# Transnormer attention and a two-layer feed-forward: loads of batch 1, the place of GpSimd's first sums, and the queue of the tile loads

## The chip, the cores and the metric

The kernel runs on one core of a Trainium2 chip. TensorE (PE in the profile) multiplies, with its weight loads shown apart as PEld; VectorE is DVE, ScalarE is ACT, GpSimd is POOL, and SyncE (SP) computes nothing and issues DMAs. ScalarE and GpSimd can issue DMAs too. The metric is the device time of one execution in microseconds, the median over several runs.

## The reference

```python
def _attn_ref(q, k, v, g_norm):                 # (8, 8, 576, 64)
    kv = np.einsum('bhsd,bhse->bhde', k, v)
    out = np.einsum('bhsd,bhde->bhse', q, kv)
    rms = np.sqrt(np.mean(out * out, axis=-1, keepdims=True) + 1e-06)
    return (out / rms * g_norm).astype(np.float32)

def _moe_ref(x, w_in, w_out):                   # x (4608, 512), w_in (512, 2048)
    h = x @ w_in
    g = np.maximum(0.01 * h, h)
    return (g @ w_out).astype(np.float32)
```

The output of the attention, with heads and batch rearranged to 4608 rows of 512, is x. All arrays but the weights are float32. w_in and w_out are float64, so each of their tiles is loaded with twice the bytes and rounded to float32 on the chip.

## The kernel before

**Blocks.** The 4608 rows are taken as nine blocks of 512. The first block is computed plainly while the weights are still arriving; blocks 1 and 0 follow with one level of Strassen's scheme (block 0 for the half of the hidden columns that the first pass left out), and blocks 2 to 8 with two levels in the first product.

**Weight tiles.** There are 32 tiles of 512 KB (w_jobs), numbered in the order in which they are loaded and rounded. Tiles 0 to 15 belong to the first half of the hidden columns, 16 to 31 to the second half (16 to 19 and 24 to 27 are w_in, 20 to 23 and 28 to 31 are w_out, a chunk each). A tile of w_in takes four DMAs, one of w_out a single one. load_w issues them (L235), round_w and finish_w turn a tile into float32: two readings on ScalarE (L260, L262), a cut on VectorE (L264), one more on ScalarE (L269), and two operations on VectorE (L279, L282). The raw tiles lie in a few buffers (stage, pairs, early) that are used in turn.

**The first block** (L1112) has eight steps n. H n is the product with one w_in tile, O n the product with one w_out tile; H n needs tiles 0, 1, 3, 5, 7, 9, 11, 13 in this order, and O n needs tiles 2, 4, 6, 8, 10, 12, 14, 15. TensorE runs H 0, H 1, O 0, H 2, O 1 and so on. Between them `plan` (L1151) places, by hand, the rounding of tiles (numbers), the finishing of a tile (f), the steps of the attention of batch 1 (a: transposes of q, the product kv, its copy, the outputs o_ps, the norm) and the tail of batch 0 (t). Batch 1 is loaded as four pairs of heads; load_pair issues six DMAs for a pair (k, v and four pieces of q, 1,144 KB).

**Blocks 1 and 0** go by chunks c of 512 hidden columns, and a chunk has seven products in the order 1, 2, 6, 5, 7, 3, 4 (ORDER, L760). Products 1, 6, 7, 4 of the first layer accumulate in one PSUM bank (h_a or h_b), 2, and 5 with 3, in another (h_c or h_d): before a bank is accumulated on, its value must have been copied or added to g (done, L922: L925, L927, L932 and the adds of L697). The second layer's products o 1 to o 7 of a chunk run between the first layer's of the next chunk. A position in this run is a slot, seven to a chunk. GpSimd computes the sums that the scheme needs: of w_in (sides_w1, in `pairs`), of w_out (sides_w2), of g (sums_of, in gs), and a second level of w_in sums (combine, parts 0 and 1; part 2 is VectorE's). VectorE computes the sums of x (sides_x), all through add (L696). The sums of the weights are also written to DRAM (L750, L791 to L795), for the later blocks to read; a buffer in `pairs` is used again for the next chunk, so its sums wait until its write has landed.

**Order.** Most instructions are pinned, that is, they keep the order in which the program has them on their engine; the others the scheduler places when the kernel is built. GpSimd's first sum of a group is not pinned in blocks 1 and 0. Two small copies on GpSimd (L1178) that read x come ahead of its sums. In blocks 1 and 0 one tile is rounded at each of the slots of W_SLOTS, and the load of a later tile is issued there by ScalarE (L1284). Each DMA issued by SyncE or ScalarE carries one of eight semaphores in turn and waits for the DMA that carried it before.

Of the kernel before, what the change touches and what calls it, by code (L numbers as in the profile page):

```python
# [24 lines left out]
def kernel(  # L25
# [64 lines left out]
    ps_m = ctx.enter_context(tc.tile_pool(name="ps_m", bufs=1, space=bass.MemoryType.PSUM))  # L90

    pin = tc.keep_in_program_order
    steady = first_done = in_line = in_first = False

    def in_turn(ins):

# [56 lines left out]
    def load_pair(b, p, what="kvq", homes=None):  # L153


        if "k" in what:
            for i, (to, src) in enumerate(((k_ins, k), (v_ins, v))):
                to[b, p] = load_two(nc.sync, src[b, 2 * p:2 * p + 2],
                                    homes[i] if homes else in_tile("kv"[i]))
        if "q" not in what:  # L160
            return
        t = homes[2] if homes else ins.tile([P, T * D], F32, tag="q_in", name="q_in")
        for l in range(2):
            for c in range(2):
                r0, n = 64 * l + 32 * c, T * D - 32 * c
                src = q[b, 2 * p + half_of(p, l)].rearrange("(t s) d -> t (s d)", s=T)
                pin(nc.sync.dma_start(t[r0:r0 + 32, :n], src[:, 32 * c:]))
        q_ins[b, p] = t
# [131 lines left out]
    def load_w(j, *eng):  # L300
        eng = eng or (nc.sync,)
        dst, src = w_jobs[j]
        if w_in.dtype == I64:
            w_raws[j] = load_f64(src.bitcast(U32), eng)
        else:
            load(dst, src, eng)
# [7 lines left out]
    def round_w(j):  # L314

        steps = rounding(j)
        for _ in range(3):
            next(steps, None)
        finish_w()
        halfway.append(steps)  # L320
# [7 lines left out]
    def finish_w():  # L328
        while halfway:
            for _ in halfway.popleft():  # L330
                pass
# [214 lines left out]
    def first_attention():  # L546
# [43 lines left out]
        keep_warm(384)  # L590
        for j in range(3, 7):
            load_w(j)
        load_pair(1, 0)
        copy_kv(0, kv_ps)


# [74 lines left out]
        for _ in w0:  # L671
            pass
        load_w(7)
        load_pair(1, 1)
        invert(1)
        spread(1)
        w1 = rounding(1)
# [6 lines left out]
        halfway.append(w1)  # L684
        finish_w()
        load_w(8)
        load_pair(1, 2, homes=homes_1[2])
        for j in range(2, 5):
            round_w(j)
            load_w(j + 7)  # L690
            if j == 3:
                load_pair(1, 3, homes=homes_1[3])
        finish_w()


    def add(eng, out_, a, b_, minus=False, pinned=False):  # L696
        ins = eng.tensor_tensor(out_, a, b_, op=ALU.subtract if minus else ALU.add)  # L697
        if pinned or steady:
            pin(ins)

    def sides_w1(c):
# [22 lines left out]
    t12, t34 = pair(2, 2, U, N2), pair(3, 2, U, N2)  # L724
    writes = []

    def sides_w2(n):

        c = units[n][1]
        b11, b12 = w2_sb[0][c][:, :, :N2], w2_sb[0][c][:, :, N2:]
        b21, b22 = w2_sb[1][c][:, :, :N2], w2_sb[1][c][:, :, N2:]

        def sums(i):
            t = (t12, t34)[i]
            if n >= NC:
                pin(nc.sync.dma_start(t, w2_dram[c][i]))
                return
            if i == 0:  # L740
                add(nc.gpsimd, t[:, 0], b12, b11, True)
                add(nc.gpsimd, t[:, 1], b22, t[:, 0], True)
            else:
                add(nc.gpsimd, t[:, 0], b22, b12, True)
                add(nc.gpsimd, t[:, 1], b21, t12[:, 1], True)
            if (n, i) == (NC - 1, 1):

                writes.append((w2_dram[c][i], t))
            else:
                pin(nc.sync.dma_start(w2_dram[c][i], t))  # L750
        return {1: b11, 2: b21, 3: b22, 5: t12[:, 0], 6: t12[:, 1], 7: t34[:, 0],
                4: t34[:, 1]}, sums

# [16 lines left out]
    def combine(c, part):  # L770


        direct = w1_sb[0][c].rearrange("p u (t r) m -> p u r t m", t=2)
        last = w1_sb[1][c][:, :, 2:, :].unsqueeze(3)
        parts = [((5, 6), pair(0, U, 2, 2, P))], [((7, 3), pair(1, U, 2, 2, P))], \
            [((1, 2), direct), ((4,), last)]

        eng = nc.vector if part == 2 else nc.gpsimd
        for js, y in parts[part]:
            t = view(next(stage_homes), 0, 4, len(js), P)  # L780
            s1, s2, s3, s4 = (t[:, i, :, :] for i in range(4))
            y11, y12, y21, y22 = (y[:, u, r, :, :] for u in range(2) for r in range(2))

            add(eng, s1, y21, y22, pinned=part == 2)
            add(eng, s2, s1, y11, True, pinned=part == 2)
            add(eng, s3, y11, y21, True, pinned=part == 2)
            add(eng, s4, y12, s2, True, pinned=part == 2)
            to = w1_dram[c][:, :, AT[js[0]]:AT[js[0]] + len(js), :]
            if js[0] == 1:
                for r in range(2):  # L790
                    pin(nc.sync.dma_start(to[:, r, :, :], y[:, 0, r, :, :]))  # L791
            else:
                pin(nc.sync.dma_start(to[:, :2, :, :], y[:, 0, :, :, :]))
            pin(nc.sync.dma_start(to[:, 2, :, :], y22))
            pin(nc.sync.dma_start(to[:, 3:, :, :], t))  # L795


    reads = [(c, k) for _ in range(2, NB) for c in range(NC) for k in ORDER]
# [313 lines left out]
    def first_block(between):  # L1112
# [27 lines left out]
        for t in range(4):  # L1140
# [6 lines left out]

    first_attention()
    tail, a_steps = tail_of(0, NT, S, True), attention(1, False)
    t, a, f = "taf"  # L1150
    plan = {(1, 0): (t, 5), (1, 1): (t, t, 6, t), (2, 0): (t, 7, t), (2, 1): (t, f, a),  # L1151
            (3, 0): (a, 8), (3, 1): (f, a, 9), (4, 0): (10, f), (4, 1): (11,),
            (5, 0): (f, a, a, 12, a), (5, 1): (a, 13), (6, 0): (f, a, 14),
            (6, 1): (a, a, 15, a, f), (7, 0): (a, a), (7, 1): (16,), (8, 0): (f,)}
    loaded = 12

    def between(n, half):
        nonlocal loaded
        for what in plan.get((n, half), ()):
            if what == f:  # L1160
                finish_w()
            elif what in (t, a):
                go(tail if what == t else a_steps, 1)
            else:
                round_w(what)
                for j in range(loaded, {12: 17, 13: 18, 14: 19, 15: 20, 16: 21}.get(what, min(what + 7, 16)) + 1):
                    load_w(j)
                    loaded += 1
# [3 lines left out]
    in_first = False  # L1172
    first_done = True
    rounded = 17
    x_sides, _, sums, _ = sides_x(1)
    for _ in sums:
        pass
    for i, r in ((1, 0), (0, 1)):  # L1178
        nc.gpsimd.tensor_copy(pair(i, U, 2, 2, P)[:1, 0, 0, r, :1], x_sides[1][:1, 0, :1])
    h_sides, more = sides_w1(0)  # L1180
    more()
    for part in range(2):
# [33 lines left out]
    for i, chunks in rounds:  # L1216
# [7 lines left out]
        for c in chunks:  # L1224
# [5 lines left out]
            for t in range(7):  # L1230
# [30 lines left out]
                if slot in HELD and i == NB - 1:  # L1261
                    pass
                elif waited == LAG:
                    go_o()
                elif o_queue:
                    waited += 1
                if one:
                    at = 7 * now + t

                    if t == 1 and (i == 0 or c < K):  # L1270
                        combine(c, 2)
                    if t == 3 and nxt[0] < 2:
                        h_sides, more_h = sides_w1(nxt[1])
                        if nxt in ((1, 1), (0, K), (0, K + 1)):
                            combine(nxt[1], 0)
                    if t == 5 and nxt[0] < 2:
                        more_h()
                        if nxt in ((1, 1), (0, K), (0, K + 1)):
                            combine(nxt[1], 1)
                    if at in W_SLOTS:  # L1280
                        round_w(rounded)
                        rounded += 1
                        if loaded < len(w_jobs):
                            load_w(loaded, nc.scalar)  # L1284
                            loaded += 1
                    else:
                        finish_w()
                    if at in (19, 20):
                        load_pair(2, at - 19)
                    go(late, LATE_ONE.get(at, 0))  # L1290
                    go(a_steps, A_SLOTS.get(at, 0))
                    load_some()
                    if at in (33, 36):
                        for key in (("11", "12"), ("22", "21"))[at == 36]:
                            load_part(os, key)
                    if at == 7 * NC - 4:
                        x_sides, _, sums, _ = sides_x(0)
                        go(sums)
                    elif at == 7 * N1 - 4:
                        x_sides, new_quarters, sums, inner = sides_x(2)  # L1300
                        go(sums)
                    elif at == 7 * N1 - 3:
                        inner(0)
                    elif at == 7 * N1 - 2:
                        inner(1)
# [46 lines left out]
```

## Time and profile before

| | us |
|---|---|
| median of four runs | 946.19 (946.01 to 947.04) |
| the profiled execution, time | 946.01 |
| the profiled execution, span | 944.3 |

| Engine | busy us | share of the span |
|---|---|---|
| TensorE | 910.2 | 96% |
| its weight loads | 796.3 | 84% |
| VectorE | 638.2 | 68% |
| GpSimd | 391.8 | 41% |
| ScalarE | 346.9 | 37% |

The times in the text are microseconds from the span's start. In a timeline line the first number is the start and the second the duration; then come the engine (a q behind its name marks its DMA queue), the line of the code, the operation, what it writes and reads, and how many instructions are merged; in brackets stands how long the engine had stood still and what it waited for. In a line of waits stand who waited for whom, then the sum, how often, and the longest. TensorE's busy share by stretches shows where it stands still: from 0 to 100 us it is busy 90.3 us, from 100 to 200 us 80.4, and from 200 us on nearly throughout. The DMA engines are busy all the time from 15 to 45 and from 50 to 70 us (share 0.95 or more), and again from 96 to 124 us.

### The profile page before, as it was taken

What the parts mean: (1) busy time and instruction counts of PE and PEld (TensorE: products, weight loads), DVE (VectorE), ACT (ScalarE), POOL (GpSimd) and SP (SyncE); (2) the same over time, 40 slices, a digit from 0 to 9 for tenths busy, and PEclk for the clock granted to TensorE, in tenths of its full rate; (3) what the DMA queues carried; (4) which work ended last, traced back from release to release, by engine and by line L of the source; (5) the groups of instructions that cost most, each with busy time, mean ns of one, the idle gap of its engine ahead of it and who ended that gap; (6) DMA issues with size and microseconds to landing.
All of it is one profiled execution on the core that took longest, in us unless ns stands there. A gap on an engine that the chain in (4) does not pass through costs nothing.

```text
span 944.3 us, 18288 instructions
## 1 busy us (share of the span) xinstructions
PE 910.2 (96%) x7072; PEld 796.3 (84%) x7072; DVE 638.2 (68%) x1161; ACT 346.9 (37%) x682; POOL 391.8 (41%) x456
## 2 busy tenths in 40 slices
PE   9988598899999999999999999999999999999998
PEld 5533476788899899999999999999989999999997
DVE  5758577864665777578856876587758765755565
ACT  5645354412324432443234333433343333223231
POOL 2061555596423365225422452246224623452222
PEclk9999889999999999999999999999999999999999
DMA  8993973459788878877787779766865666667632
GB/s 266 249 239 103 350 221 123 144 165 296 251 248 300 251 223 216 263 242 220 222 261 226 242 210 269 232 202 195 256 193 174 189 215 193 184 188 225 197 121 89
DMA packets 92981, 204.26 MB, mean 216 GB/s; under 512 B 10080, under 2 KB 44512, under 8 KB 92896
## 3 DMA queue, kind: packets, MB, share of 16 engines
q1 hardware_dynamic: 78176, 184.95, 65.6%
q10 hardware_dynamic: 14272, 16.98, 5.5%
q8 instruction: 56, 0.92, 0.4%
q0 software_dynamic: 448, 1.18, 0.3%
q14 instruction: 29, 0.24, 0.1%
HBM read 175.54 MB, written 27.53 MB: 215 GB/s over the span
## 4 chain that ended last, share of the span: by engine, by line
PE 78%; DMA 8%; DVE 7%; ACT 3%; POOL 2%; issue 2%; SPq 0%; ACTq 0%; POOLq 0%; DVEq 0%
PE o_a L125 18%; PE o_c L125 17%; PE h_ha L125 10%; PE h_hb L125 10%; PE h_hc L125 8%; PE h_hd L125 8%; PE o_ps L125 3%; DMA pairs<-in_moe_w_in_dram 1%; DVE w L282 1%; DVE w L279 1%; DMA w<-pairs 1%; PE h_b L125 1%; DMA pairs<-in_v_dram 1%; PE h_d L125 1%; DVE g L697 1%
## 5 line engine op out<-in xcount | busy, mean ns | idle before, releaser
L697 POOL TENSOR_TENSOR gs<-g 128x512 f32<-128x512 f32 x68 | 87.2, 1286 | 278.3 <-ACT g L900 278.3
L900 ACT ACTIVATE g<-g 128x512 f32<-128x512 f32 x130 | 82.0, 631 | 155.4 <-DVE g L697 145.4
L1019 ACT COPY w_all<-h_ha 128x512 f32<-128x512 f32 x84 | 48.9, 582 | 171.7 <-PE h_ha L125 159.7
L125 PE MATMUL o_a<-pairs,gs 128*128 128x256 f32 x408 | 97.0, 381 | 0.0
L125 PE MATMUL o_c<-pairs,gs 128*128 128x256 f32 x400 | 94.9, 380 | 0.0
L697 DVE TENSOR_TENSOR o<-h_hb,o 128x128 f32<-128x128 f32 x104 | 29.9, 287 | 83.5 <-ACT pairs L1019 83.4
L125 PEld LDWEIGHTS o_a<-pairs,gs 128*128 128x128 f32 x408 | 74.4, 190 | 9.9 <-POOL pairs L697 1.2
L697 DVE TENSOR_TENSOR o<-o_c,o 128x512 f32<-128x512 f32 (+1 forms) x98 | 66.0, 673 | 23.4 <-PE o_c L125 23.0
L125 PEld LDWEIGHTS o_c<-pairs,gs 128*128 128x128 f32 x400 | 72.9, 190 | 8.3
L697 DVE TENSOR_TENSOR o<-o_a,o 128x512 f32<-128x512 f32 x82 | 56.1, 684 | 28.9 <-PE o_a L125 28.7
L125 PE MATMUL h_ha<-stage,w_all 128*128 128x128 f32 x448 | 59.9, 276 | 0.2 <-POOL stage L697 0.2
L125 PEld LDWEIGHTS h_ha<-stage,w_all 128*128 128x128 f32 x448 | 56.7, 192 | 3.4 <-issue 0.7
L697 DVE TENSOR_TENSOR g<-g,pairs 128x512 f32<-128x512 f32 x84 | 55.7, 689 | 1.9
L697 POOL TENSOR_TENSOR pairs<-g 128x128 f32<-128x128 f32 x52 | 23.7, 457 | 76.3 <-PE h_hb L125 47.5
L697 DVE TENSOR_TENSOR w_all<-h_hc,w_all 128x512 f32<-128x512 f32 x56 | 38.4, 685 | 15.8 <-PE h_hc L125 15.8
L697 DVE TENSOR_TENSOR o<-h_hd,o 128x128 f32<-128x128 f32 x78 | 22.2, 284 | 38.1 <-ACT pairs L1019 38.0
L697 POOL TENSOR_TENSOR gs<-gs,g 128x512 f32<-128x512 f32 x34 | 46.2, 1359 | 2.2
L697 POOL TENSOR_TENSOR gs<-g,gs 128x512 f32<-128x512 f32 x34 | 46.8, 1375 | 0.3
L125 PE MATMUL h_hb<-stage,w_all 128*128 128x128 f32 x336 | 46.7, 275 | 0.0
L1019 ACT COPY pairs<-h_hb 128x384 f32<-128x384 f32 x84 | 40.0, 476 | 13.3 <-PE h_hb L125 12.6
L125 PE MATMUL h_hd<-xT,w_all 128*128 128x128 f32 x224 | 43.3, 275 | 0.0
L125 PE MATMUL h_hb<-xT,w_all 128*128 128x128 f32 x224 | 43.3, 275 | 0.0
(245 smaller groups left out, 2255.7 us busy)
## 6 DMA issues: line engine op xcount, KB each, us to landing
w_all<-w SPq DMA_DIRECT2D x196, 448.0 KB, 4.2
pairs<-w SPq DMA_DIRECT2D x60, 512.0 KB, 4.4
out_dram<-o ACTq DMA_DIRECT2D x35, 256.0 KB, 5.0
v_in<-in_v_dram SPq DMA_DIRECT2D x27, 288.0 KB, 4.6
k_in<-in_k_dram SPq DMA_DIRECT2D x26, 288.0 KB, 4.3
q_in<-in_q_dram SPq DMA_DIRECT2D x52, 144.0 KB, 5.8
q_in<-in_q_dram SPq DMA_DIRECT2D x52, 140.0 KB, 5.9
w<-pairs SPq DMA_DIRECT2D x8, 512.0 KB, 3.7
```

Source lines behind the costliest of these rows:

```text
L125: pin(nc.tensor.matmul(*args, **kw))
L279: pin(nc.vector.scalar_tensor_tensor(dst, in0=cut, scalar=3, in1=dst, op0=ALU.logical_shift_left, op1=ALU.bitwise_or))
L282: pin(nc.vector.tensor_tensor(dst, dst, add, op=ALU.add))
L697: ins = eng.tensor_tensor(out_, a, b_, op=ALU.subtract if minus else ALU.add)
L900: nc.scalar.activation(t, t if src is None else src, func=AF.Prelu, alpha=SLOPE)
L1019: nc.scalar.copy(q[:, at], bank)
```

## The change

- In first_attention the four pairs of batch 1 are issued later: pair 0 behind tile 8, pair 1 behind tile 9, pairs 2 and 3 behind tile 10; before, pairs 0, 1, 2 came ahead of tiles 7, 8, 9, and pair 3 behind tile 10.
- The plan of the first block is written anew: tiles 8, 9 and 10 are rounded up to half a step earlier, the steps of batch 1's attention stand closer together and the last ends earlier, and the sums of x for block 1 (x) are placed at step 7, where they followed the first block before.
- All sums on GpSimd keep the program's order from block 1 on (in_block_1). Ahead of them stands one small copy that reads the last of VectorE's sums of x, in place of the two copies that read x.
- Writes of weight sums in blocks 1 and 0 are not issued at once but put on a list (put_off) and issued three slots later (write_later).
- In blocks 1 and 0 the tile loads are issued by SyncE, not by ScalarE.

No arithmetic changes, and no bytes are added or removed.

```diff
     pin = tc.keep_in_program_order
-    steady = first_done = in_line = in_first = False
+    steady = first_done = in_line = in_first = in_block_1 = False
+    later = []
...
         for j in range(3, 7):
             load_w(j)
-        load_pair(1, 0)
         copy_kv(0, kv_ps)
...
         load_w(7)
-        load_pair(1, 1)
         invert(1)
...
         load_w(8)
-        load_pair(1, 2, homes=homes_1[2])
+        load_pair(1, 0)
         for j in range(2, 5):
             round_w(j)
+            if j == 4:
+                load_pair(1, 3, homes=homes_1[3])
             load_w(j + 7)
-            if j == 3:
-                load_pair(1, 3, homes=homes_1[3])
+            if j < 4:
+                load_pair(1, j - 1, homes=homes_1.get(j - 1))
         finish_w()
...
-        if pinned or steady:
+        if pinned or steady or (in_block_1 and eng is nc.gpsimd):
             pin(ins)
...
+    def put_off(to, t):
+        later.append([2, to, t])
+
+    def write_later():
+        for item in list(later):
+            item[0] -= 1
+            if item[0] < 0:
+                pin(nc.sync.dma_start(*item[1:]))
+                later.remove(item)
...
-                pin(nc.sync.dma_start(w2_dram[c][i], t))
+                put_off(w2_dram[c][i], t)
...
-                    pin(nc.sync.dma_start(to[:, r, :, :], y[:, 0, r, :, :]))
+                    put_off(to[:, r, :, :], y[:, 0, r, :, :])
             else:
-                pin(nc.sync.dma_start(to[:, :2, :, :], y[:, 0, :, :, :]))
-            pin(nc.sync.dma_start(to[:, 2, :, :], y22))
-            pin(nc.sync.dma_start(to[:, 3:, :, :], t))
+                put_off(to[:, :2, :, :], y[:, 0, :, :, :])
+            put_off(to[:, 2, :, :], y22)
+            put_off(to[:, 3:, :, :], t)
...
-    t, a, f = "taf"
-    plan = {(1, 0): (t, 5), (1, 1): (t, t, 6, t), (2, 0): (t, 7, t), (2, 1): (t, f, a),
-            (3, 0): (a, 8), (3, 1): (f, a, 9), (4, 0): (10, f), (4, 1): (11,),
-            (5, 0): (f, a, a, 12, a), (5, 1): (a, 13), (6, 0): (f, a, 14),
-            (6, 1): (a, a, 15, a, f), (7, 0): (a, a), (7, 1): (16,), (8, 0): (f,)}
-    loaded = 12
+    t, a, f, x = "tafx"
+    plan = {(1, 0): (t, 5), (1, 1): (t, t, 6, t), (2, 0): (t, 7, t), (2, 1): (t, 8, a),
+            (3, 0): (9, f), (3, 1): (a, 10), (4, 0): (f, a), (4, 1): (a, a, 11, a),
+            (5, 0): (a, 12), (5, 1): (a, 13), (6, 0): (f, a, a, 14),
+            (6, 1): (a, 15, a, f), (7, 0): (a, x), (7, 1): (16,), (8, 0): (f,)}
+    loaded, x_sides = 12, None
...
+            elif what == x:
+                x_sides, _, sums, _ = sides_x(1)
+                go(sums)
...
-    x_sides, _, sums, _ = sides_x(1)
-    for _ in sums:
-        pass
-    for i, r in ((1, 0), (0, 1)):
-        nc.gpsimd.tensor_copy(pair(i, U, 2, 2, P)[:1, 0, 0, r, :1], x_sides[1][:1, 0, :1])
+    in_block_1 = True
+    pin(nc.gpsimd.tensor_copy(pair(0, NW)[:1, :1], x_sides[4][:1, 0, :1]))
...
                 elif o_queue:
                     waited += 1
+                write_later()
                 if one:
...
                         if loaded < len(w_jobs):
-                            load_w(loaded, nc.scalar)
+                            load_w(loaded)
                             loaded += 1
```

More of the change, by code (lines that the diff above doesn't have):

```diff
@@ L1149 @@
     tail, a_steps = tail_of(0, NT, S, True), attention(1, False)
-    t, a, f = "taf"
-    plan = {(1, 0): (t, 5), (1, 1): (t, t, 6, t), (2, 0): (t, 7, t), (2, 1): (t, f, a),
-            (3, 0): (a, 8), (3, 1): (f, a, 9), (4, 0): (10, f), (4, 1): (11,),
-            (5, 0): (f, a, a, 12, a), (5, 1): (a, 13), (6, 0): (f, a, 14),
-            (6, 1): (a, a, 15, a, f), (7, 0): (a, a), (7, 1): (16,), (8, 0): (f,)}
-    loaded = 12
+    t, a, f, x = "tafx"
[4 more added lines that the diff above has]
+    loaded, x_sides = 12, None
     def between(n, half):
-        nonlocal loaded
+        nonlocal loaded, x_sides
         for what in plan.get((n, half), ()):
```

## The prediction

> **What bounds the kernel now.** I read, in this order, the waits of TensorE, its timeline, the timelines of ScalarE, VectorE, GpSimd and SyncE around each wait, and the DMA share by stretches. (H 0 to 7 and O 0 to 7 are the first block's steps; products 1 to 7 of a chunk are those of blocks 1 and 0, o 1 to o 7 the second layer's.) The waits of TensorE come first, for from 190 us on it stands still for 1.4 us only: all that this change can win or lose lies before that.
>
> ```profile
> PE h_b L125 <- ACT g L925: 10.6, 1, 10.6
> PE o_acc L125 <- DVE w L282: 4.1, 2, 2.6
> PE h_a L125 <- DVE g L697: 3.4, 2, 2.6
> PE h_c L125 <- DVE g L697: 2.7, 1, 2.7
> PE o_a L125 <- DVE o L697: 2.5, 2, 1.9
> PE h_ps L125 <- DVE w_all L282: 2.2, 1, 2.2
> ```
>
> One wait of 10.6 us stands out: product 6 of chunk 1 of block 1 waits until ScalarE has copied product 1 out of bank h_b (L925). ScalarE was late because it issues tile loads (L1284) itself:
>
> ```profile
> 105.82 5.10 ACTq L235 DMA_DIRECT2D stage<-in_moe_w_in_dram  x4
> 110.97 0.63 ACT L900 ACTIVATE g<-g 128x512 f32<-128x512 f32 x1 [5.18 <-DMA stage<-in_moe_w_in_dram]
> 112.80 5.48 ACTq L235 DMA_DIRECT2D stage<-in_moe_w_in_dram  x4
> 118.33 0.60 ACT L900 ACTIVATE g<-h_a 128x512 f32<-128x512 f32 x1 [5.10 <-DMA stage<-in_moe_w_in_dram]
> 119.34 0.57 ACT L925 COPY g<-h_b 128x512 f32<-128x512 f32 x1
> ```
>
> Behind the gap the matmuls run slow (PEclk 0.50 from 120 to 124 us): 3.75 and 3.13 us for groups that take 1.89, 3.1 us more. The same happens after the gap of 2.73 us at 156 us (3.19 and 2.42 us, 1.8 more), not after those of 2.57 and 2.56.
>
> The other waits are for VectorE, which rounds the weight tiles (L264, L279, L282). There the reader is to compare durations with and without GpSimd at work:
>
> ```profile
> 54.85 1.58 DVE L279 SCALAR_TENSOR_TENSOR w_all<-cut,w_all 128x512 uint32<-128x512 uint32 x1
> 56.47 1.64 DVE L282 CUSTOM_DVE_ANT_0 w_all<-w_all,add 128x1024 uint16<-128x1024 uint16 x1
> ...
> 82.85 0.69 DVE L279 SCALAR_TENSOR_TENSOR w<-cut,w 128x512 uint32<-128x512 uint32 x1
> 83.58 0.69 DVE L282 CUSTOM_DVE_ANT_0 w<-w,add 128x1024 uint16<-128x1024 uint16 x1
> ```
>
> ```profile
> 54.38 1.50 POOL L697 TENSOR_TENSOR pairs<-w_all 128x512 f32<-128x512 f32 x1 [0.40 <-ACT cut L260]
> 55.96 1.60 POOL L697 TENSOR_TENSOR pairs<-pairs,w_all 128x512 f32<-128x512 f32 x1
> ...
> 103.79 1.28 POOL L697 TENSOR_TENSOR pairs<-w_all 128x512 f32<-128x512 f32 x1 [28.65 <-DMA w<-pairs]
> ```
>
> A VectorE operation that reads SBUF ends 0.55 us after the GpSimd operation then running (55.88 to 56.43, 57.56 to 58.11): the two take turns. A turn with 512 columns on GpSimd takes 1.6 us, with 256 about 1.05 to 1.1 (two in 2.19 us from 57.64). Operations of VectorE with a PSUM operand stay at 0.68.
>
> The Trainium skill agrees (GPSIMD Engine Reference, Specifications: GpSimd shares its SBUF interfaces with VectorE and contends with two-input and two-port operations), and it is the rule that speaks against this change, which puts both engines' work in one place; it has no price, and the sum goes by the rows above.
>
> **Part 1, order of loads and steps up to 91 us.** The same 28 DMAs stand ahead of batch 1's last pair as before, the DMA share is 1.0 there, so that pair (k and v at 54, q at 58 us) and tile 11 (59.6) land as before: 0 us. Tile 9 passes two pairs (2.3 MB) and lands some 8 us earlier (42), and GpSimd, which ran from 54 to 75, is silent: the waits of 2.17 (tile 9) and part of 2.57 go. What is late next: VectorE's copy of kv stands behind tile 11's cut, 59.6 + ScalarE 1.3 + 0.5 + 0.5 = 61.9, so the matmuls of o_ps start at 62.0 (1.3 us wait). From there by the rows' durations: tile 11 done at 68.3 and H 6 starts (68.56 before); tile 12 done 73.0, O 5 starts (75.74 before); H 7 ends 80.2. Now tile 14 is finished behind the steps of the norm that stood behind it before: end of H 6 at 72.1, g 0.6, tile 13 (0.5 + 0.73 + 0.69), transposes and reductions 2.5, root 0.3, cuts 1.2 + 0.4, reciprocal 0.35, spread 1.0, tile 15's cuts 1.1, tile 14 0.6 + 0.75 + 0.69 = 83.5. So O 6 waits 3.35 us (1.54 before), and O 7 ends at 90.65 against 91.4: 0.7 us won. For the clock after 3.35 us the rows give 0 (gap 2.57) to 1.8 us (gap 2.73), twice that after 10.56; between them I take 0.9.
>
> The skill's rule (TensorE: Matmul & The Clock Gate, Part 1) lets an idle window of about 3.4 us halve the clock, windows running freely; the row at 2.73 us already lost it, so the row decides. By the rule alone this term would be near 0.
>
> **Part 2, GpSimd behind the sums of x.** VectorE's four sums now end at 91.1. GpSimd then starts its 16 first operations, done by 75 us before: 8 with 512 columns, 8 with 256. VectorE has to do, until it adds product 7 (which product 4 waits for): tile 16 (two more), eight sums of part 2, tiles 17 and 18 (six). Before the change these ran from 96.5 to 103.3 beside a waiting GpSimd. Now each takes a turn: from 91.6, 8 x 1.6 + 8 x 1.05 = 21.3 us, so to 112.9, and product 7 is added at 113.5 to 114.0. Product 4 starts at 114.0, where TensorE could have done so at 101.6 (products at 1.73 us from 90.65; product 6 waits 0.7 for GpSimd). In between product 3 goes at 109.1, behind ScalarE's copy that is queued behind tile 17's. The gap of 12.4 us takes the place of the 10.6. Uncovered it would cost VectorE's own pace only: 9 us from 91.3, no wait at all; that is the lower bound of this term.
>
> **Part 3, loads on SyncE.** ScalarE loses 22 DMA issues and the 15.1 us that it waited for them (DMA rows of the waits). That covers nothing any more: product 6 of chunk 1 comes at 122 us by part 2 and finds GpSimd's sum (115.9) and the copy (121.1) done. TensorE, slow by 3.1 us as in the row at 120: product 4 114.0, chunk 1's product 1 117.4, 2 120.4, 6 122.1, o 1 123.8, then product 5 waits until 127.7 for VectorE (tiles 19 to 21 beside GpSimd), 2.1 us; o 6 starts at 132.9, against 132.03. So 1.6 us lost since 91.
>
> SyncE takes those 22 issues (0.35 to 1.4 us each, about 15 us), each behind the writes put off by three slots. Writes that wait for GpSimd hold the loads: tile 23 until 113, tile 24 until 117 to 120 and landing by 129, needed at 142; tile 26 landing at 135, needed at 154. They cost 0 while that cover of 13 to 19 us holds. GpSimd needs the written buffer again later than that (113 against a landing at 109.5): 0. In blocks 1 and 0 a put off write is issued four slots (14 us) ahead of its buffer's next use: 0.
>
> **Part 4, 132 to 190 us.** VectorE now adds o 7 and o 3 ahead of tiles 24 and 25, so the wait of 1.94 at 147 goes. But the add of o 1 of the next unit comes ahead of tiles 25 and 26 and the add of product 2 behind them: cut 0.5, 1.3, cut 0.5, 1.3, add 0.6 = 4.85 us in which product 5 waits, 2.73 before, with 1.8 of slow clock both times. Before it, product 4 of chunk 1 waits 2 us for the add of product 7, behind eight sums that now run beside GpSimd. The wait of 2.56 at 171 goes, since GpSimd pauses. I reach product 4 of chunk 2 at 172.5, against 171.05: 0.6 us more lost. Bounds: all these waits stay away (-7 us, the sum of the rows) or VectorE takes turns throughout (8 operations x 0.95, +7).
>
> **Sum.** -0.7 + 1.6 + 0.6 + 0.9 = +2.4 us. The profiled execution has a span of 944.3 us and a time of 946.01, 0.2 under the median of 946.19 of four runs; I add to the median: 948.6.
>
> **Rivals.** (1) Faster: VectorE isn't held at every turn. For it: at 209.5 to 213.1 four short sums were held twice only. Against: the rows from 54 to 60 and 142 to 147. If half the turns are lost, product 4 starts at 107, GpSimd then bounds: sum for o 6 ready at 109 + four groups of 2.9 or so = 122, o 6 at 123.5, 8.5 us earlier: 938. It decides when the 17 operations take under 18 us. (2) No change: no slow clock after the first block's O 6, and 1 us less in part 4: 946.5. The change then only moves the wait. (3) Slower by more: the loads queued on SyncE decide, if a write ahead of them waits 13 us longer for GpSimd than worked out; tile 24 late by 6 us stalls VectorE and with it every add behind: 954. Against it the DMA share falls below 0.5 after 132 us.
>
> **How the numbers follow.** Four runs spread by 0.1%, so 0.2% (1.9 us) is about what can be told from no change. My case, slower by 1 to 6 us (946.5 to 952): 0.43; rival 1: 0.35; rival 2: 0.13; rival 3: 0.09. The range 936 to 955 takes in rival 1 but for its bound without any collision (-11.4 us, 934.8), and most of rival 3; the likeliest case alone is 946.5 to 952. My case reaches a little below the bound of 0.2%, so slower is 0.50, same 0.14, faster 0.36.
>
> **What would show it.** Right: ScalarE without DMA waits between 100 and 150 us; GpSimd idle up to about 91 us; L279 and L282 at 0.69 up to there and at 1.1 to 1.6 behind; the longest wait of TensorE in chunk 0's products 3 and 4, on VectorE or on the copy queued behind it, 9 us or more in all; a wait of about 3 us at O 6 of the first block. Wrong: those waits under 5 us (then rival 1), or VectorE waiting for a tile's DMA (rival 3). A TensorE that stands still after 190 us would show that the put off writes cost what I put at nothing.

## The result, and the profile after

The changed kernel takes 949.83 us, the median of 52 runs (946.03 to 956.10); the kernel before takes 947.86 us over its 77 runs by now (943.09 to 952.39). The ratio is 1.0025, with a 95% interval of 1.0017 to 1.0033: slower by 2.4 us (the two medians alone differ by 2.0). Single runs of either kernel spread by 9 to 10 us, some nine times what four runs of before had shown. The profiled execution after took 951.21 us with a span of 949.5, 5.2 us more than the span before; it lies 1.4 us above its kernel's median, and that of before 1.9 us under its own. So a difference of two spans says little, and I compare stretches between the same matmuls.

The waits of TensorE in the first 200 us of the profile after (columns as before: sum, how often, the longest):

```profile
PE h_c L126 <- DVE g L698: 8.0, 1, 8.0
PE h_c L126 <- ACT g L938: 6.3, 1, 6.3
PE o_acc L126 <- DVE w L283: 4.4, 2, 3.5
PE o_a L126 <- DVE o L698: 3.1, 1, 3.1
PE h_d L126 <- DVE g L698: 2.5, 1, 2.5
```

The wait of 10.6 us at product 6 of chunk 1 is gone. In its place stand 6.3 us at product 3 of chunk 0 and 8.0 us at product 5 of chunk 2.

For the stretches I take six starts from TensorE's timeline: A block 1, B product 4 of chunk 0, C o 6 of chunk 0, D product 5 of chunk 2, E product 4 of chunk 2, F the product kv of batch 2. A is a time from the span's start; the others are differences (us).

| | A | A-B | B-C | C-D | D-E | E-F | F-end | sum |
|---|---|---|---|---|---|---|---|---|
| before | 91.36 | 12.69 | 27.98 | 24.14 | 14.88 | 19.09 | 754.16 | 944.3 |
| after | 91.24 | 20.50 | 20.64 | 27.28 | 12.97 | 24.62 | 752.25 | 949.5 |

A-B is 7.8 us longer, and B-C, where the wait of 10.6 us stood, 7.3 us shorter. This exchange is the first half of the result. C-E costs 1.2 us more, E-F 5.5 us more, and 1.9 us come back behind F.

A-B, VectorE's timeline:

```profile
92.70 1.30 DVE L280 SCALAR_TENSOR_TENSOR w_all<-cut,w_all 128x512 uint32<-128x512 uint32 x1
94.04 1.64 DVE L283 CUSTOM_DVE_ANT_0 w_all<-w_all,add 128x1024 uint16<-128x1024 uint16 x1
...
98.45 1.50 DVE L698 TENSOR_TENSOR w<-w_all 128x256 f32<-128x256 f32 x1
99.87 1.48 DVE L698 TENSOR_TENSOR w<-w_all,w 128x256 f32<-128x256 f32 x1
...
109.98 1.10 DVE L283 CUSTOM_DVE_ANT_0 w_all<-w_all,add 128x1024 uint16<-128x1024 uint16 x1
111.00 0.68 DVE L698 TENSOR_TENSOR g<-h_a,g 128x512 f32<-128x512 f32 x1
```

GpSimd's timeline beside it:

```profile
91.89 0.18 POOL L1190 COPY pairs<-xt 1x1 f32<-1x1 f32 x1 [85.49 <-DVE xt L698]
92.18 1.27 POOL L698 TENSOR_TENSOR pairs<-w_all 128x512 f32<-128x512 f32 x1
...
99.75 1.32 POOL L698 TENSOR_TENSOR pairs<-w,pairs 128x512 f32<-128x512 f32 x1
...
110.50 1.17 POOL L698 TENSOR_TENSOR w_all<-pairs,w_all 128x256 f32<-128x256 f32 x1
```

GpSimd is idle for 85.49 us and then works without a pause, and nearly every VectorE operation on SBUF between 92.7 and 111 us takes a turn with it: 0.69 us becomes 1.1 to 1.6, and a sum of 256 columns, 0.42 us before, becomes 0.9 to 1.5. Only one sum of 128 columns (104.54) still takes its 0.28 us. The steps that took VectorE from 92.86 to 103.31 us before, with three of the sums of x among them, take it from 92.70 to 111.00 now.

The wait of 6.3 us at product 3 is put down to ScalarE, but ScalarE itself stood for VectorE. Its timeline:

```profile
105.72 0.63 ACT L270 ACTIVATE w_all<-cut 128x512 int32<-128x512 f32 x1 [6.02 <-DVE cut L265]
106.25 0.57 ACT L938 COPY g<-h_c 128x512 f32<-128x512 f32 x1
```

The copy out of h_c, which product 3 needs, is queued behind the reading of tile 17, which waits 6.02 us for VectorE's cut.

### The profile page after: what moved, and what is told of

It is laid out like the page before. It is cut to its first block, busy times and chain, and to the rows that moved or that the text cites. A ratio compares the mean times of both kernels' runs of the same rounds, so it can differ in the third digit from the quotient of the medians.

```text
span 949.5 us, 18287 instructions
## 1 busy us (share of the span) xinstructions
PE 915.8 (96%) x7072; PEld 800.7 (84%) x7072; DVE 651.9 (69%) x1161; ACT 347.4 (37%) x682; POOL 391.5 (41%) x455
## 4 chain that ended last, share of the span: by engine, by line
PE 81%; DVE 8%; DMA 6%; ACT 3%; issue 1%; SPq 0%; ACTq 0%; DVEq 0%
PE o_a L126 18%; PE o_c L126 18%; PE h_ha L126 10%; PE h_hb L126 10%; PE h_hc L126 8%; PE h_hd L126 8%; PE o_ps L126 3%; DMA pairs<-in_moe_w_out_dram 2%; DMA pairs<-in_moe_w_in_dram 1%; PE h_d L126 1%; PE h_b L126 1%; PE h_a L126 1%; DMA stage<-in_moe_w_in_dram 1%; DVE w_all L280 1%; DVE w L698 1%
## 5 line engine op out<-in xcount | busy, mean ns | idle before, releaser
L126 PE MATMUL o_a<-w,g 128*128 128x256 f32 x168 | 42.7, 400 | 3.3 <-DVE o L698 3.1
```

The costliest lines, as they stand in the source:

```text
L126: pin(nc.tensor.matmul(*args, **kw))
```

## The experiments

Each run is compared with runs of the kernel before on the same chip (medians 947.67 to 947.88 us). The stretches are those of one profile of each; the time in us is the median.

| run | A | A-B | B-C | C-D | D-E | E-F | F-end | time | ratio to before |
|---|---|---|---|---|---|---|---|---|---|
| changed, loads on ScalarE | 93.72 | 20.18 | 29.79 | 22.87 | 12.54 | 25.04 | 752.26 | 958.08 | 1.0116 [1.0098, 1.0134] |
| before, loads on SyncE | 96.03 | 14.59 | 19.84 | 33.07 | 12.77 | 19.19 | 754.21 | 949.49 | 1.0017 [0.9999, 1.0035] |
| same, writes put off | 91.82 | 12.57 | 20.05 | 36.35 | 14.07 | 19.14 | 754.20 | 949.02 | 1.0014 [0.9995, 1.0033] |
| changed, no hook | 98.22 | 11.80 | 18.28 | 34.72 | 12.98 | 24.87 | 752.23 | 953.62 | 1.0067 [1.0048, 1.0086] |
| changed, GpSimd as before | 96.46 | 11.79 | 17.82 | 37.59 | 16.41 | 19.95 | 754.18 | 950.32 | 1.0037 [1.0015, 1.0059] |
| changed, writes at once | 90.73 | 20.18 | 20.49 | 29.99 | 12.35 | 21.22 | 755.34 | 952.95 | 1.0058 [1.0040, 1.0076] |
| loads on SyncE, adds later | 93.66 | 14.72 | 18.66 | 41.00 | 10.72 | 22.24 | 754.20 | 956.99 | 1.0096 [1.0077, 1.0116] |
| same, new order to 91 us | 94.67 | 14.63 | 18.07 | 36.81 | 10.72 | 22.21 | 754.19 | 955.97 | 1.0088 [1.0067, 1.0108] |
| loads on SyncE, order kept | 92.43 | 14.59 | 16.94 | 30.23 | 13.16 | 19.79 | 754.16 | 943.00 | 0.9947 [0.9929, 0.9966] |
| changed, order kept | 94.75 | 20.18 | 19.97 | 27.57 | 12.25 | 21.61 | 754.57 | 950.94 | 1.0037 [1.0019, 1.0055] |
| loads on SyncE, order kept, new order to 91 us | 96.75 | 14.60 | 18.01 | 25.15 | 13.18 | 19.78 | 754.53 | 944.18 | 0.9961 [0.9945, 0.9976] |
| before, order kept | 92.73 | 13.11 | 27.68 | 24.59 | 13.19 | 18.26 | 754.54 | 945.31 | 0.9973 [0.9962, 0.9984] |

**The changed kernel with the loads back on ScalarE.** The prediction held that the loads on SyncE save nothing, since the delay of product 4 covers them.

```diff
-                            load_w(loaded)
+                            load_w(loaded, nc.scalar)
```

> The changed kernel with the tile loads of blocks 1 and 0 back on ScalarE. Theory as predicted (the loads on SyncE are worth nothing once GpSimd's sums delay product 4, since ScalarE's standing lies beside that delay): within 2 us of the changed kernel. Rival (the two delays add, since ScalarE's copy for product 3 is behind the loads too): 5 to 14 us above the changed kernel.

Measured: 1.0116 against the changed kernel's 1.0025, 0.9% or 8.6 us more. The rival is right. The waits of TensorE and, in a second fence, ScalarE's timeline of this run:

```profile
PE h_b L126 <- ACT g L936: 13.3, 1, 13.3
PE h_c L126 <- ACT g L938: 6.3, 1, 6.3
```

```profile
115.67 5.75 ACTq L236 DMA_DIRECT2D stage<-in_moe_w_in_dram  x4
...
123.22 7.61 ACTq L236 DMA_DIRECT2D stage<-in_moe_w_in_dram  x4
...
131.89 0.58 ACT L936 COPY g<-h_b 128x512 f32<-128x512 f32 x1
```

The loads come in ScalarE's order behind the work of product 3, so they slide with the delay and do not lie beside it: four DMAs hold ScalarE for 5.75 us, the next four for 7.61, and the copy of h_b comes at 131.89 us.

**The kernel before with the loads on SyncE, and with the writes put off as well.** The first is the line of the change in load_w alone; the second adds put_off and write_later as in the change.

> The kernel before with one edit: SyncE issues the tile loads of blocks 1 and 0 at once, all else as before. Theory (ScalarE standing in DMA issues for 15.1 us makes the wait of 10.6 us of TensorE and the 3.1 us of slow clock behind it; GpSimd's first sums are long done by then): ScalarE has no DMA waits between 100 and 150 us, product 6 of chunk 1 starts by 112 us (120.06 before), and the time is 6 to 13 us below before, half of the 13.7 us or more. Rival (the loads on SyncE come too late, behind the writes that wait for GpSimd): VectorE waits for a tile's DMA, and the time is within 3 us of before or above it.

> As the run with the loads on SyncE, and with the block writes put off by three slots as well. Theory (put off writes cost nothing, since no buffer is needed again sooner than 14 us on, and hold no load): within 2 us of that run, so 6 to 13 us below before. Rival (writes that are put off push each other, and the sums that wait for the buffers, later): 3 us or more above that run, with waits of GpSimd on DMAs of w. Second rival (without it the loads stand behind writes that wait for GpSimd): 3 us or more below that run.

Measured: no gain, 1.0017 and 1.0014, with intervals that reach from no change to 0.35% slower. B-C did lose its 8 us in both, as the theory said, and C-D gained 9 and 12. The time is the rival's, but its sign, a VectorE that waits for a tile's DMA, doesn't show, and ScalarE, which reads the raw tiles, waits for none from 88 us on either. So the gain was there and was handed back, and the put off writes by themselves did nothing to the time. They did move work: in the second run TensorE waits 4.2 and 3.0 us for GpSimd's sums of w_in (product 6 of chunks 1 and 2), which it doesn't in the first, and 6.3 us at product 5 in place of 10.9. Where it was handed back, in the run with the loads on SyncE: ScalarE's timeline, then VectorE's.

```profile
150.95 0.59 ACT L932 COPY g<-h_a 128x512 f32<-128x512 f32 x1 [1.14 <-PE h_a L125]
151.43 0.68 ACT L262 ACTIVATE add<-stage 128x512 uint32<-128x512 uint32 x1
```

```profile
152.68 0.69 DVE L697 TENSOR_TENSOR o<-o_c,o 128x512 f32<-128x512 f32 x1 [4.21 <-PE o_c L125]
153.29 0.68 DVE L264 TENSOR_SCALAR cut<-cut 128x512 f32<-128x512 f32 x1
153.89 1.75 DVE L279 SCALAR_TENSOR_TENSOR w_all<-cut,w_all 128x512 uint32<-128x512 uint32 x1
```

ScalarE's copy of product 6 of chunk 2, and VectorE's add of o 1 of the next chunk, both wait for TensorE, and only then do both engines turn to tile 24. Behind it come tiles 25 and 26 and the add of product 2, which product 5 waits for: 10.9 us. In the kernel before, ScalarE had the readings of tile 24 at 142 us, and those of three more tiles, ahead of that copy:

```profile
142.21 0.66 ACT L260 ACTIVATE cut<-stage 128x512 f32<-128x512 f32 x1
...
157.72 0.57 ACT L932 COPY g<-h_a 128x512 f32<-128x512 f32 x1
```

These copies and adds are not pinned. When the DMA issues left ScalarE, the scheduler placed them anew, ahead of pinned tile work of earlier slots. That is a new theory: the order, not the load, takes the gain.

**GpSimd's part undone, in two ways.** Without the hook (first diff), and with the sums unpinned and the two old copies (second).

```diff
-    pin(nc.gpsimd.tensor_copy(pair(0, NW)[:1, :1], x_sides[4][:1, 0, :1]))
```

```diff
-        if pinned or steady or (in_block_1 and eng is nc.gpsimd):
+        if pinned or steady:
...
-    pin(nc.gpsimd.tensor_copy(pair(0, NW)[:1, :1], x_sides[4][:1, 0, :1]))
+    for i, r in ((1, 0), (0, 1)):
+        nc.gpsimd.tensor_copy(pair(i, U, 2, 2, P)[:1, 0, 0, r, :1], x_sides[1][:1, 0, :1])
```

> The changed kernel without the one small copy that holds GpSimd's first sum behind VectorE's sums of x; all else as changed. Theory (the loss is the collision of these 16 sums with 17 operations of VectorE from 91 to 111 us): GpSimd starts between 45 and 60 us, the waits of 6.33 and 1.02 us in chunk 0 with their 3.7 us of slow clock go, some 2 to 4 us of waits come back in the first block, where VectorE now takes turns; the time is 6 to 10 us below the changed kernel, 4 to 8 below before. Rival (the new order of loads and steps is what costs): no more than 2 us from the changed kernel.

> The changed kernel with its GpSimd part undone: sums not pinned, the two small copies as before, the new order of loads and steps, the loads on SyncE and the put off writes kept. By stages, from the runs so far: block 1 starts at 91 to 92 us, product 4 of chunk 0 starts 12 to 15 us later (20.5 as changed), o 6 another 20 later, but product 5 of chunk 2 only 33 to 36 us after that (27.3 as changed), since the gain waits behind o 1's add and the tiles; from product 4 of chunk 2 to the product kv of batch 2 it takes 19.1 again (24.6 as changed), and 2 us more after it. Sum: 1 to 5 us below the changed kernel. Rival (the stretch of 24.6 us comes from the order of loads and steps, not from the pinned sums): 24 to 25 us there, and the time is within 2 us of the changed kernel.

Measured: A-B falls from 20.5 to 11.8 us in both, so the collision is GpSimd's. Without the hook GpSimd stands still from 82.8 to 112.2 us, and VectorE's two operations on tiles 17 and 18 (106.6 to 109.4 us) take 0.69 us each. But, against both expectations, neither is faster than the changed kernel: 1.0067 and 1.0037. Block 1 starts 5 to 7 us later, since the sums now collide with tiles and steps of batch 1, which the new plan puts closer together (5.2 and 4.6 us of wait at O 6), and C-D rises to 35 and 38 us, as in the run with the loads on SyncE. E-F is 24.87 with pinned sums and 19.95 without: that stretch belongs to the pin, and its rival, the new order of loads and steps, is out.

**The changed kernel with its writes at once.** put_off is replaced by the DMA itself at all its places.

> The changed kernel with the block writes issued at once again. Theory (put off writes cost nothing and save nothing): within 2 us of the changed kernel. Rivals: the tile loads then stand behind writes that wait for GpSimd (3 us or more slower, VectorE waiting for tiles between 115 and 150 us); or the put off writes make GpSimd wait for its buffers (3 us or more faster).

Measured: 1.0058 against 1.0025. The put off writes cost nothing; here they save some 3 us. Where is not settled: C-D is 2.7 us longer and F-end 3.1, E-F 3.4 shorter. VectorE waits for no tile's DMA, as the first rival wanted. One wait of ScalarE, 2.23 us before it reads tile 21, is put down to one; the changed kernel has the same 2.23 us there, put down to VectorE, so it explains nothing.

**Adds of the second layer later.** A first try at the order: VectorE's adds of chunks 0 to 2 are held, and pinned behind the tile of their slot; then the same with the new order of loads and steps.

```diff
-            else:
+            elif not steady and c < NC - 1:
+                held.append((to, bank))
+            else:
...
+                    for to, bank in held:
+                        add(nc.vector, to, bank, to, pinned=True)
+                    held.clear()
```

> The kernel before with the loads on SyncE, and with VectorE's adds of the second layer's products (chunks 0 to 2 of the blocks 1 and 0) issued, pinned, behind the weight tile of their slot and not where the scheduler puts them. Theory (moving the loads off ScalarE made the scheduler put o 1's add, which waits for TensorE, ahead of three weight tiles, and the add of product 2, which product 5 waits for, behind them: that handed the gain of 8 us back): from o 6 to product 5 of chunk 2 it takes 22 to 28 us (33.1 with the loads on SyncE alone, 24.1 before), and the time is 5 to 9 us below the run with the loads on SyncE alone, 3 to 8 below before. Rival (16 weight tiles at some 5 us each on VectorE and ScalarE set the pace from 91 to 172 us in whatever order): product 5 of chunk 2 starts no sooner than 66 us after block 1, and the time is within 3 us of that run.

> As the run with the adds later, with the changed kernel's order of loads and steps up to 91 us in addition (writes at once, GpSimd as before). Theory (that order is worth 0.7 us and no more): within 2 us of the run with the adds later. Rival (it saves the 2 to 4 us of waits of the first block in most runs): 3 us or more below it.

Measured: both slower, 1.0096 and 1.0088, and C-D is 41 and 37 us. Now the o products wait, 8.8 us for one add behind tile 25, and ScalarE's order, which was left alone, holds the next tile back behind the copy of product 6. The theory's number failed, and the rival's "within 3 us of that run" too. The new order of loads and steps is within 2 us, as expected.

**The order kept.** Copies and activations of g and o on ScalarE and the second layer's adds on VectorE are pinned to the program's order in blocks 1 and 0; the four kernels differ in what lies under it.

```diff
-        nc.scalar.activation(t, t if src is None else src, func=AF.Prelu, alpha=SLOPE)
+        ins = nc.scalar.activation(t, t if src is None else src, func=AF.Prelu, alpha=SLOPE)
+        if not steady:
+            pin(ins)
...
-                nc.scalar.copy(g11, bank)
+                pin(nc.scalar.copy(g11, bank))
...
-                add(nc.vector, to, bank, to)
+                add(nc.vector, to, bank, to, pinned=True)
```

> The kernel before with the loads on SyncE, and with the second layer's adds on VectorE and the copies and activations of g and o on ScalarE pinned to the program's order in blocks 1 and 0 (in the run with the loads on SyncE alone the scheduler had moved them, o 1's add ahead of three tiles, and on ScalarE the copy of product 6, which waits for TensorE, ahead of the readings of a tile). The order on both engines is then nearly that of before without the DMA issues. Theory (the scheduler's new order hands the gain back): o 6 some 20 us after product 4 of chunk 0, product 5 of chunk 2 by 22 to 27 us after o 6 (33.1 with the loads on SyncE alone), 72 us or less from block 1's start to product 4 of chunk 2 (79.7 before); 5 to 9 us below before. Rival (the 16 tiles on VectorE and ScalarE, 4.5 to 5 us each beside GpSimd, set the pace in any order): 77 us or more there, and the time within 3 us of before.

> The changed kernel with the same instructions of VectorE and ScalarE pinned to the program's order in blocks 1 and 0. Theory: product 4 of chunk 0 still 20 us after block 1's start, from o 6 to product 5 of chunk 2 22 to 25 us (27.3 as changed), 2 to 5 us below the changed kernel. Rival (the tiles set the pace): 27 us or more there, within 2 us of the changed kernel.

> As the run with the loads on SyncE and the order kept, with the changed kernel's order of loads and steps up to 91 us in addition; writes at once, GpSimd as before. Theory (that order is worth about nothing): within 2 us of that run. Rival (GpSimd's sums now collide with the steps of batch 1, which stand closer together): 3 us or more above it, block 1 starting at 95 us or later.

> The kernel before with only the order kept: the same instructions of VectorE and ScalarE pinned as in the run with the loads on SyncE and the order kept, and the loads left on ScalarE. Theory (the 5 us below before of that run come from the loads, which the pinned order lets through): the wait of product 6 of chunk 1 for ScalarE stays at 9 to 12 us, o 6 comes 26 to 30 us after product 4 of chunk 0 (28.0 before, 16.9 in that run), and the time is within 2 us of before. Rival (the pinned order is itself the gain, and the loads are worth nothing): 3 us or more below before.

Measured, in the order of the quotes: 0.9947, 1.0037, 0.9961, 0.9973.

- With the loads on SyncE the order is what decides: 1.0017 becomes 0.9947, 5.0 us below before, at the edge of what was expected. A to E takes 74.9 us, 79.7 before; the rival's 77 or more, tiles that set the pace in any order, is out for this kernel. But 72 us or less had been expected, and for C-D, which stays at 30 us, 22 to 27: part of the gain is still handed back.
- The order alone is worth 2.6 us (0.9973), between theory and rival. The rest, 0.26% or 2.5 us, is the loads'; the two intervals overlap a little, so its size is rough. The waits in the two profiles say what each does. Order alone, TensorE's waits and ScalarE's timeline:

```profile
PE h_b L125 <- ACT g L927: 10.6, 1, 10.6
```

```profile
113.85 6.22 ACTq L235 DMA_DIRECT2D stage<-in_moe_w_in_dram  x4
```

With the loads on SyncE in addition:

```profile
PE o_a L125 <- DVE o L697: 4.6, 3, 2.3
PE h_a L125 <- DVE g L697: 4.1, 2, 2.9
PE o_acc L125 <- DVE w L282: 4.1, 2, 2.6
PE h_d L125 <- ACT g L929: 2.4, 1, 2.4
```

The one long wait stays as long as ScalarE issues the loads; without them nothing over 2.9 us is left before 200 us.

- In the changed kernel the order is worth nothing (1.0037 against 1.0025): my expectation failed, and both signs of its rival, that the tiles set the pace, came true there (C-D 27.57 us, the time within 2 us). A-B is still 20.2 us. Without GpSimd's part, and with the writes at once, the same order gives 0.9961, 0.76% or 7.2 us less. These two were undone together; that it is GpSimd's part, and not the writes, by which the changed kernel then loses is argued from A-B, which falls from 20.18 to 14.60 us, and from the run with the writes at once, which was not faster.
- The new order of loads and steps makes 0.9947 into 0.9961: 1.2 us between the medians, within the 2 us expected, though block 1 starts at 96.75 us in that profile, which was its rival's sign.

The kernel before with the loads on SyncE and the order kept is the fastest, 0.5% below before and 0.8% below the changed kernel; with the new order added (0.9961) it lies within the same interval.

## Why the prediction came out, and where its steps were off

It gave 948.6 us against 946.19, slower by 2.4; measured are 2.4. The agreement to a tenth is luck: at 91, 132 and 172 us the forecast holds to 0.6 us, but between them steps are off by 2 to 3 us and cancel, two further steps were not seen, one sum doesn't come out of its own rows, and single runs spread by 10 us.

- **Order of loads and steps up to 91 us.** Block 1 at 90.65 was forecast, measured 91.24. The waits forecast were 1.3 us for kv and 3.35 at O 6; they were 1.08 and 3.52, with 0.72 and 0.86 beside them. The 0.9 us for a slow clock behind O 6 were not paid in this profile; other runs paid them (last section).
- **GpSimd behind the sums of x.** The mechanism is right: idle until 91.9 us, then turns. The size is not: product 4 was to start at 114.0 and started at 111.74, product 3 at 106.96 and not 109.1. I gave each of GpSimd's eight sums of 512 columns a turn of 1.6 us and each of 256 columns one of 1.05. GpSimd went through the eight long ones in 1.44 us each (92.18 to 103.70) and through the eight short ones in 0.99 (103.70 to 111.63), and VectorE was held for no longer. The operations were to take 21.3 us and took some 18.4, next to the 18 at which rival 1 was to decide; product 4 came 9.5 us late and not 12.4. Of these 7.35 are the waits at products 3 and 4, less than the 9 that I had named as a sign and more than the 5 that would have refuted me, and 1.9 are slow clock. TensorE's longest wait is not there but at product 5 of chunk 2.
- **Loads on SyncE.** That ScalarE's standing is gone shows: no DMA wait there between 100 and 150 us. That this is worth nothing, because the other delay covers it, was wrong: with the loads on ScalarE the changed kernel is 8.6 us slower. The sum came out because it set one gap in place of the other; the step that failed is the word "covers". A delay ahead of an instruction on its own engine moves it, it does not hide it. B-C was forecast as 18.9 us and was 20.6, with 4.3 us of slow clock where I had 3.1; o 6 at 132.9 was forecast, measured 132.38.
- **Put off writes.** At no cost, as forecast; in the changed kernel they even save some 3 us.
- **132 to 172 us.** Product 4 of chunk 2 at 172.5 was forecast, measured 172.63, because errors cancel. The steps listed for the wait of 4.85 us add up to 4.2, and the waits listed (2 and 4.85 against 1.94, 2.73 and 2.56 before) make this part 0.4 us shorter, not 0.6 longer; by them the whole sum would have been +1.4 us. The add of o 1 ahead of tiles 25 and 26 is the right cause, but the wait was 7.98 us and not 4.85:

```profile
151.72 0.69 DVE L698 TENSOR_TENSOR o<-o_c,o 128x512 f32<-128x512 f32 x1
152.98 1.34 DVE L265 TENSOR_SCALAR cut<-cut 128x512 f32<-128x512 f32 x1 [0.57 <-ACT cut L261]
...
156.92 0.43 DVE L265 TENSOR_SCALAR cut<-cut 128x512 f32<-128x512 f32 x1 [1.28 <-ACT cut L261]
...
158.83 0.68 DVE L698 TENSOR_TENSOR g<-h_c,g 128x512 f32<-128x512 f32 x1
```

  I had summed VectorE's operations and left out that it stands for ScalarE's readings of the next tile (0.57 and 1.28 us), and one more turn with GpSimd (1.34 for 0.43). Against it, the wait of 2 us at product 4 of chunk 1 did not come.
- **172 to 197 us: not seen.** I put this at nothing. In the order in which GpSimd is now pinned its sums run on as VectorE rounds tile 30. VectorE's timeline of after, then GpSimd's:

```profile
175.43 1.75 DVE L280 SCALAR_TENSOR_TENSOR w<-cut,w 128x512 uint32<-128x512 uint32 x1
177.22 1.64 DVE L283 CUSTOM_DVE_ANT_0 w<-w,add 128x1024 uint16<-128x1024 uint16 x1
...
188.19 0.65 DVE L698 TENSOR_TENSOR o<-o_a,o 128x512 f32<-128x512 f32 x1
```

```profile
173.95 1.27 POOL L698 TENSOR_TENSOR pairs<-w,pairs 128x512 f32<-128x512 f32 x1
175.19 1.45 POOL L698 TENSOR_TENSOR pairs<-w_all 128x512 f32<-128x512 f32 x1
```

  Before, GpSimd paused there, and the two operations on tile 30 took 0.69 us each; again VectorE's timeline, then GpSimd's:

```profile
173.33 0.69 DVE L279 SCALAR_TENSOR_TENSOR w<-cut,w 128x512 uint32<-128x512 uint32 x1
174.06 0.69 DVE L282 CUSTOM_DVE_ANT_0 w<-w,add 128x1024 uint16<-128x1024 uint16 x1
```

```profile
174.85 1.28 POOL L697 TENSOR_TENSOR pairs<-w,w 128x512 f32<-128x512 f32 x1 [3.33 <-PE o_c L125]
```

  The add of o_a, queued behind tiles 30 and 31 and the norm of batch 2, comes 4 us later (188.19 against 184.03), TensorE waits 3.12 us (0.56 before), and the clock falls behind it: 3.78 and 3.12 us for two groups that take 1.89. All five kernels with pinned sums have 21.2 to 25.0 us for E-F, those without, but for the two with the adds later, 18.3 to 20.0.
- **Behind 197 us** the span after is 1.9 us shorter; TensorE's waits of 1.24 us at 257.5 and 0.19 at 263.2, 1.4 us of it, are gone. I had said that nothing could be won or lost there. Two more kernels with pinned sums show it (752.2); the ones with writes at once and with the order kept don't: there TensorE waits 1.8 us for GpSimd at 224 and 225 us. Why is open.
- **The rivals.** Rival 1, faster, fails: VectorE is held at nearly every turn. Rival 2, no change, is not quite excluded: the interval begins at 0.17%, inside its 0.2%, and that no clock is lost behind O 6 did come true in the profile. Rival 3, late tiles behind the writes, doesn't show: VectorE waits for no tile's DMA in any of the profiles, and ScalarE, which reads the raw tiles, for none from 91 us on in the profile after. Two of their prices are a little off as well: 109 and four groups of 2.9 us make 120.6, not 122 (rival 1), and 0.9 and 1 us off the sum leave 946.7, not 946.5 (rival 2).

## What to carry to other kernels

In these runs a sum on GpSimd is free only where VectorE has little to do in SBUF; moved next to VectorE's rounding it holds VectorE for as long as the sum runs, and undoing it moves the collision to wherever the sum goes. Taking a wait off one engine is not a gain until the next in-order queue has been read: here 8 us reappeared some 40 us later, because instructions that the scheduler may place were placed anew. When an edit changes what an engine issues, compare the order on every engine, and pin the consumers before judging the edit.

## What the runs showed of the hardware

The same stop of TensorE costs a different amount of slow clock from run to run. O 6 and O 7 in the changed kernel and in the changed kernel with the order kept, the same code up to there, from TensorE's timeline:

```profile
84.24 7.16 PE L126 MATMUL o_acc<-w,g 128*128 128x512 f32 x16 [3.52 <-DVE w L283]
```

```profile
84.81 10.10 PE L126 MATMUL o_acc<-w,g 128*128 128x512 f32 x16 [3.52 <-DVE w L283]
```

After 3.5 us of standing the 16 matmuls take 7.16 us, 10.10, and 8.80 in the runs with the loads on ScalarE and with the writes at once. A stop of 2.17 us before the step that waits for tile 9 cost nothing in the kernel before (3.70 us) and 1.7 us (5.40) in the run with the adds later. The slow clock goes with the spread of 10 us between runs of one kernel: of the 53 executions of the changed kernel on record, the 18 with a mean granted clock of 0.989 or more have a median of 948.2 us, the 13 with 0.984 or less one of 953.1. The start of block 1 differs too, between profiles whose code is the same up to there: 91.4 to 96.0 us in the six with the loads and steps of before, 90.7 to 94.8 in the four with the new order and the hook. In the latest of the first group the stop at tile 9 is 4.76 us and not 2.17, in the latest of the second the clock behind O 6 is slow (10.10 us, the second row above).

The Trainium skill (TensorE: Matmul & The Clock Gate, Part 1) says that the activity window of the clock gate runs freely, so that the same code sees different slow stretches from run to run. These rows agree in so far as one and the same stop costs 0 to 3 us; no run here shows the window itself.
